# Sixteen products of ones ahead of the first scores, and a new order of the first 329 steps, in a fused attention and MLP kernel

## The chip, the cores and the metric

The kernel runs on one core of a Trainium2 chip. The core has five engines with a queue of instructions each, worked off in order: TensorE (PE in the profile) multiplies matrices, VectorE (DVE) and ScalarE (ACT) work on elements, GpSimd (POOL) does what is left, and SyncE (SP) issues the transfers between device memory and the core. An instruction that waits holds up everything behind it on its own engine, and nothing on the others. The metric is the time of one execution on the device in microseconds (us); the kernel before takes 593.65 us, the median of three runs from 591.35 to 593.74.

## The reference

An attention over a narrow band of keys and over block summaries, followed by a two-layer MLP with an exact GELU. There are 4 batches, 8 heads, 768 positions and a head size of 64:

```python
k_sum = k.reshape(B, H, nb, block, D).max(axis=3)        # block = 32
v_sum = v.reshape(B, H, nb, block, D).mean(axis=3)
scores_l = scale * np.matmul(q, k.transpose(0, 1, 3, 2))
mask_l = np.abs(pos[:, None] - pos[None, :]) < window    # window = 16
scores_s = scale * np.einsum('bhsd,bhnd->bhsn', q, k_sum) + np.log(block)
scores_all = np.concatenate([np.where(mask_l, scores_l, -1e9), scores_s], axis=-1)
a = np.exp(scores_all - np.max(scores_all, axis=-1, keepdims=True))
a = a / (np.sum(a, axis=-1, keepdims=True) + 1e-09)
x = np.matmul(a, np.concatenate([v, v_sum], axis=2))     # then (3072, 512)
h = x @ w_in                                             # (512, 2048)
out = (0.5 * h * (1 + erf(h / sqrt(2)))) @ w_out         # (2048, 512)
```

The attention's inputs are 32-bit floats; the two weights arrive as 64-bit floats.

## The kernel before, in words

**The work and its stages.** The attention is cut into 24 units, one for each batch, each third of the positions (256 queries) and each half of the heads (4). Two units make up a chunk of 256 rows for the MLP, so that there are 12 chunks. For the matrix products most operands are split into two 16-bit parts, "hi" and "lo", and three 16-bit products stand for one 32-bit product; units 0 to 5 do their attention in 32-bit products instead. Chunks from the fifth on compute the first layer with a Strassen scheme, and the last two chunks the second layer too.

**The order.** Nothing is planned at run time. The string `ORDER` lists 1653 steps by name, with the unit, chunk or weight block they work on; the kernel calls them one after the other, and each step appends its instructions to the queues of its engines. So the order of the list is the order on each engine's queue, SyncE's included, and instructions wait only where they need a result or a free buffer. The rest of this section names the steps that the change moves.

**The weights.** `fetch_w_in i` (line 346) brings a block of `w_in`, 1 MB of 64-bit floats. VectorE makes 32-bit floats of it by operations on bits, three to a block (`wi_bits`, lines 361, 366, 370), ScalarE the hi part (`wi_hi`, L396). The lo part comes either from VectorE (`wi_lo`, L399) or from TensorE, which subtracts by two products into PSUM (`wi_diff`, L407 and L408), and ScalarE copies it out (`wi_dlo`, L413). Block 5 also gets its Strassen differences early (`wt_add`, L424 and L430, on VectorE, then `wt_hi`, L435, on ScalarE and `wt_lo`, L438, on VectorE). `w_out` is treated alike (`wo_bits`, `wo_hi`, `wo_lo`).

**The keys and the block means.** `fetch_k b g` (L485) brings keys for the block maxima; `prep_k` (L494, VectorE) takes the maxima, `prep_k_end` (L502, L503) splits them, and `k_sums` (L507, ScalarE) spreads them. `sum_vt` (L521, TensorE) sums the values of batch 0 over blocks, and `mean_vt` (L528) copies the means out.

**One unit.** `load_q` (L566), `load_k`, `load_v` fetch. `k_pack` (L618, L620, ScalarE) lays keys and maxima side by side. `f_mask` (L607, TensorE) writes the mask into PSUM by four products, and `f_scores` (L631) adds 16 products of 32 bit to it, which the trace shows as 32 instructions. `evac` (L736, ScalarE) copies the scores out, `maximum` (L749, GpSimd) takes the largest over the partitions, `shift` (L754, VectorE) subtracts it, `exponent` (L757, ScalarE) follows, and TensorE makes the sums (`f_sums`, L653) and the values (`f_values`, L645). VectorE divides (`norm_take` L822, `norm_rec` L827 and L828, `norm_spread` L832, `norm_mult` L839), ScalarE takes the hi part (`x_hi`, L843) and VectorE the lo part (`x_lo`, L846). There is one PSUM buffer for scores and one for sums and values, one buffer for q, two for values, and four work buffers of 4 KB (tag `f4k`) which keys, scores, maxima and weights share.

**The MLP.** `phase1 c i` (L866 to L868, TensorE) multiplies chunk c with weight block i in 24 products; `gelu` (L875) and `g_hi` (L878) run on ScalarE, `g_lo` (L884) on VectorE; `phase2` (L983 to L985) multiplies with `w_out`. `phase1 0 ...` is the first step that needs both units of chunk 0, and `phase1 2 0` needs units 4 and 5.

## Time and profile before

| | |
|---|---|
| runs of the kernel before | 591.35, 593.65, 593.74 us (median 593.65) |
| the profiled execution | 591.23 us |
| its span, from the first instruction to the last | 589.4 us |
| TensorE busy | 570.1 us, 97% of the span |
| VectorE busy | 462.7 us, 78% |
| ScalarE busy | 360.6 us, 61% |
| GpSimd busy | 87.9 us, 15% |
| the chain of work that ended last, by engine | PE 86%, DVE 9%, DMA 2% |

A busy time is the time in which at least one instruction of the engine runs. Matmuls overlap in the pipeline, so a busy TensorE need not be at its peak rate: the spacing of the starts tells more than the duration of one. In a row of the timeline stand the start, the time that the group took, engine, line, operation, what is written and read, and in brackets the idle time ahead of it and what ended it. "SPq" is a transfer's issue on SyncE. Rows with "x32" stand for that many instructions.

### The profile page before, as it was taken

What the parts mean: (1) busy time and instruction counts of PE and PEld (TensorE: products, weight loads), DVE (VectorE), ACT (ScalarE), POOL (GpSimd) and SP (SyncE); (2) the same over time, 40 slices, a digit from 0 to 9 for tenths busy, and PEclk for the clock granted to TensorE, in tenths of its full rate; (3) what the DMA queues carried; (4) which work ended last, traced back from release to release, by engine and by line L of the source; (5) the groups of instructions that cost most, each with busy time, mean ns of one, the idle gap of its engine ahead of it and who ended that gap; (6) DMA issues with size and microseconds to landing.
All of it is one profiled execution on the core that took longest, in us unless ns stands there. A gap on an engine that the chain in (4) does not pass through costs nothing.

```text
span 589.4 us, 13159 instructions
## 1 busy us (share of the span) xinstructions
PE 570.1 (97%) x5676; PEld 389.8 (66%) x5676; DVE 462.7 (78%) x647; ACT 360.6 (61%) x533; POOL 87.9 (15%) x41
## 2 busy tenths in 40 slices
...
GB/s 282 360 311 294 297 171 181 232 183 153 156 67 142 86 77 136 72 128 77 126 30 94 98 82 94 57 62 34 80 40 10 14 19 19 2 19 18 1 1 72
DMA packets 28794, 64.49 MB, mean 109 GB/s; under 512 B 2752, under 2 KB 7616, under 8 KB 28736
## 3 DMA queue, kind: packets, MB, share of 16 engines
...
HBM read 55.58 MB, written 6.29 MB: 105 GB/s over the span
## 4 chain that ended last, share of the span: by engine, by line
PE 86%; DVE 9%; DMA 2%; ACT 1%; issue 1%; POOL 1%; SPq 0%; POOLq 0%; DVEq 0%; ACTq 0%
PE psy L937 15%; PE pso L983 12%; PE pso L984 12%; PE pso L985 12%; PE psz L937 7%; PE psx L937 4%; PE pso_y L1148 4%; PE psh L866 4%; PE psh L867 3%; PE psh L868 3%; PE psv L802 3%; PE pss L726 2%; PE pss_x L1148 2%; PE psv L815 2%; DMA w_out_l<-in_mask_dram 1%; DMA w_out_l<-in_kp_dram 1%
## 5 line engine op out<-in xcount | busy, mean ns | idle before, releaser
L749 POOL PARTITION_ALL_REDUCE m<-s x24 | 82.1, 3422 | 341.0 <-DVE s L740 149.8
L983 PE MATMUL pso<-w_out_h,gg 128*128 128x512 f16 x320 | 121.4, 379 | 0.0
L984 PE MATMUL pso<-w_out_l,gg 128*128 128x512 f16 x320 | 121.3, 379 | 0.0
L985 PE MATMUL pso<-w_out_h,gg 128*128 128x512 f16 x320 | 121.3, 379 | 0.0
L937 PEld LDWEIGHTS <-wt 128*128 128x128 f16 x768 | 74.1, 98 | 12.3 <-issue 0.8
L866 PE MATMUL psh<-xos,ww 128*128 128x256 f16 x256 | 70.6, 276 | 0.1
L867 PE MATMUL psh<-xos,ww 128*128 128x256 f16 x256 | 70.6, 276 | 0.0
L868 PE MATMUL psh<-xos,ww 128*128 128x256 f16 x256 | 70.6, 276 | 0.0
L937 PE MATMUL psy<-xos,wt 128*128 128x256 f16 x576 | 69.8, 273 | 0.0
L937 PEld LDWEIGHTS <-ww 128*128 128x128 f16 x576 | 55.4, 98 | 14.8 <-issue 2.9
L985 PEld LDWEIGHTS <-gg 128*128 128x128 f16 x320 | 31.3, 98 | 37.7
L948 ACT ACTIVATE ww<-psy 128x512 f32<-128x512 f32 x48 | 28.0, 590 | 45.7 <-PE psy L937 43.7
L983 PEld LDWEIGHTS <-gg 128*128 128x128 f16 x320 | 31.3, 98 | 33.0 <-issue 0.4
L984 PEld LDWEIGHTS <-gg 128*128 128x128 f16 x320 | 31.3, 98 | 31.9
L969 DVE SCALAR_TENSOR_TENSOR gg<-g,gg 128x512 f16<-128x512 f32 x48 | 34.4, 730 | 11.7 <-ACT gg L965 11.5
L955 DVE TENSOR_TENSOR g<-psz,ww 128x512 f32<-128x512 f32 x24 | 16.5, 688 | 29.1 <-PE psz L937 22.9
L754 DVE TENSOR_TENSOR s<-s,m 128x1024 f32<-128x1024 f32 x24 | 29.0, 1216 | 8.9 <-POOL m L749 8.9
L962 ACT ACTIVATE g<-g 128x512 f32<-128x512 f32 x36 | 22.2, 624 | 18.2 <-DVE g L955 18.1
L757 ACT ACTIVATE s<-s 128x1024 f32<-128x1024 f32 x24 | 25.3, 1055 | 9.1 <-DVE s L754 8.8
L866 PEld LDWEIGHTS <-ww 128*128 128x128 f16 x256 | 25.4, 99 | 7.2 <-issue 2.8
L965 ACT ACTIVATE gg<-g 128x512 f16<-128x512 f32 x48 | 29.4, 623 | 1.2 <-PE pso L984 0.4
L867 PEld LDWEIGHTS <-ww 128*128 128x128 f16 x256 | 25.3, 99 | 4.6 <-issue 0.5
...
## 6 DMA issues: line engine op xcount, KB each, us to landing
...
```

The costliest lines, as they stand in the source:

```text
L749: nc.gpsimd.partition_all_reduce(out_ap=self.m32, in_ap=self.s32, channels=P, reduce_op=bass_isa.ReduceOp.max)
L754: nc.vector.tensor_tensor(out=self.s32, in0=self.s32, in1=self.m32, op=ALU.subtract)
L866: nc.tensor.matmul(ph[:, e, :], wh, xh, start=(k == 0), stop=False)
L867: nc.tensor.matmul(ph[:, e, :], wh, xl, start=False, stop=False)
L868: nc.tensor.matmul(ph[:, e, :], wl, xh, start=False, stop=(k == NCC - 1))
L937: nc.tensor.matmul(ps[:, e, :], ws, xx, start=(first and e == 0 and k == 0 and m == 0), stop=(k == 1 and m == 2), skip_group_check=True,)
L965: nc.scalar.activation(g_part(o // 2, q, 0, slice(o % 2, 4, 2)), g32t[b, q, o], AF.Copy, scale=SC_G)
L969: nc.vector.scalar_tensor_tensor(out=g_part(o // 2, q, 1, fs), in0=g32t.pop((b, q, o)), scalar=SC_G, in1=g_part(o // 2, q, 0, fs), op0=ALU ...
L983: nc.tensor.matmul(p, gh, w_out_h[:, f, :], start=(f == 0), stop=False)
L984: nc.tensor.matmul(p, gh, w_out_l[:, f, :], start=False, stop=False)
L985: nc.tensor.matmul(p, gl, w_out_h[:, f, :], start=False, stop=(f == NFC - 1))
L1148: nc.tensor.matmul(ps[:, j, :], g, ww_, start=(first and e == 0 and k == 0), stop=(e == 1 and k == 2), skip_group_check=True,)
```

## The change

It has three parts. In `setup`, `ones` (128x64, 16 bit) is set to one first instead of fourth, and TensorE gets 16 products of `ones` with itself, each 64 outputs by 512 columns, into a PSUM buffer that nobody reads; they stand at the head of TensorE's queue. The first 329 steps of `ORDER` stand in a new order; they are the same steps, and from the 330th step on the list is the same. And `prep_k` and `f_scores` get conditions with which they can serve other settings: `f_scores` can start a PSUM buffer without a mask, and `prep_k` asks by unit which batch is done in 32 bit.

In the list, wrapped anew, the lines behind the 329th step differ only in where they break. They are left out here ("...").

```diff
@@ -68,167 +68,168 @@
 N_G32 = 4
 N_OT = 1
 L2 = 5
+N_FILL = 16
 
 ORDER = '''
-fetch_k 0 0, prep_k 0 0, prep_k_end 0 0, fetch_w_in 5 5, load_m16, load_q 2, k_pack 2, f_mask 2, f_scores 2, wi_bits 5
-0, wi_bits 5 1, wi_bits 5 2, wt_add 5 0, wt_add 5 1, fetch_vt 0, wi_hi 5, load_eye, load_ind, fetch_w_in 0 0, wi_lo 5,
-k_sums 0 0, sum_vt 0, wt_add 5 2, evac 2, maximum 2, f_mask 0, load_neg, wi_bits 0 0, wi_bits 0 1, k_pack 0, wt_hi 5,
-wt_lo 5, load_q 0, f_scores 0, wi_bits 0 2, fetch_vt 1, fetch_k 0 1, prep_k 0 1, sum_vt 1, prep_k_end 0 1, shift 2,
-evac 0, maximum 0, wi_hi 0, shift 0, exponent 0, k_pack 1, exponent 2, wi_diff 0 0, fetch_vt 2, wi_diff 0 1,
-fetch_w_in 3 3, f_mask 1, load_q 1, fetch_w_in 2 2, sum_vt 2, mean_vt, load_v 0, f_sums 0, wi_bits 3 0, fetch_w_in 4
-4, wi_bits 3 1, f_scores 1, load_q 3, wi_bits 3 2, norm_take 0, wi_hi 3, s_load_vs 0, wi_diff 3 0, wi_bits 2 0,
-wi_bits 2 1, wi_bits 2 2, evac 1, wi_dlo 3 0, load_v 1, norm_rec 0, wi_hi 2, norm_spread 0, f_values 0, norm_mult 0,
-maximum 1, fetch_w_in 7 3, wi_diff 2 1, f_mask 3, wi_dlo 0 1, wi_diff 3 1, k_pack 3, x_hi 0, wi_bits 4 0, wi_bits 4 1,
-wi_dlo 0 0, x_lo 0, shift 1, exponent 1, s_load_vs 1, f_scores 3, wi_bits 4 2, f_sums 1, wi_hi 4, fetch_w_in 1 1,
-wi_bits 7 0, load_v 2, wi_bits 7 1, evac 3, f_values 1, wi_diff 2 0, wi_dlo 2 0, norm_take 1, maximum 3, norm_rec 1,
-norm_spread 1, norm_mult 1, x_hi 1, wi_bits 7 2, fetch_k 1 1, load_k 4, f_mask 4, fetch_w_out 0 4, x_lo 1, wi_dlo 2 1,
-f_sums 2, norm_take 2, prep_k 1 1, fetch_k 1 2, phase1 0 5, wi_hi 7, phase1 0 2, gelu 0 2, load_vs 2, f_values 2,
-shift 3, wi_lo 7, norm_rec 2, load_q 4, wi_lo 4, exponent 3, phase1 0 0, norm_spread 2, k_pack 4, wo_bits 0 0, wi_bits
-1 0, norm_mult 2, wo_bits 0 1, wi_bits 1 1, wo_bits 0 2, gelu 0 0, fetch_w_in 6 2, g_hi 0 0, gelu 0 5, f_scores 4,
-load_v 3, load_vs 3, wi_dlo 3 1, load_k 5, wi_bits 6 0, x_hi 2, f_sums 3, prep_k 1 2, norm_take 3, phase1 0 3, load_v
-4, wo_hi 0, x_lo 2, fetch_v 1 1, wi_bits 1 2, norm_rec 3, wo_lo 0, fetch_w_out 1 5, wi_bits 6 1, evac 4, f_values 3,
-load_q 5, prep_v 1 1, g_hi 0 5, f_mask 5, norm_spread 3, gelu 0 3, wi_hi 1, wi_bits 6 2, g_lo 0 0, norm_mult 3,
-maximum 4, fetch_k 1 0, k_pack 5, prep_k 1 0, shift 4, phase1 0 7, gelu 0 7, wo_bits 1 0, fetch_w_out 2 4, g_hi 0 7,
-wi_diff 1 0, x_hi 3, x_lo 3, exponent 4, wo_bits 1 1, g_hi 0 3, g_lo 0 3, g_hi 0 2, load_vs 4, load_mask, f_scores 5,
-g_lo 0 5, load_k 6, s_k_hi 6, fetch_k 1 3, phase1 0 4, wo_bits 1 2, g_lo 0 2, gelu 0 4, k_lo 6, phase1 1 5, fetch_v 1
-2, wi_hi 6, gelu 1 5, f_sums 4, norm_take 4, g_hi 1 5, prep_k_end 1 0, norm_rec 4, g_hi 0 4, f_values 4, g_lo 1 5,
-load_q 6, prep_k 1 3, s_q_hi 6, wo_bits 2 0, phase1 1 2, wo_hi 1, wo_lo 1, fetch_w_out 3 5, q_lo 6, wi_dlo 1 0, g_lo 0
-7, prep_v 1 2, phase1 1 0, fetch_v 1 0, wi_diff 1 1, gelu 1 0, g_lo 0 4, evac 5, maximum 5, prep_v 1 0, k_sums 1 0,
-norm_spread 4, load_v 6, wo_bits 3 0, gelu 1 2, wi_lo 6, shift 5, phase1 1 7, gelu 1 7, phase1 1 3, g_hi 1 7, wi_dlo 1
-1, exponent 5, phase1 0 1, fetch_v 1 3, norm_mult 4, wo_bits 2 1, wo_bits 3 1, load_v 5, f_sums 5, g_lo 1 7, gelu 0 1,
-g_hi 0 1, wo_bits 2 2, wo_bits 3 2, wo_hi 3, phase1 0 6, wo_hi 2, scores 6, norm_take 5, prep_v 1 3, x_hi 4,
-fetch_w_out 4 4, g_lo 0 1, phase1 1 4, load_vs 5, g_hi 1 2, g_hi 1 0, gelu 1 4, g_hi 1 4, load_q 7, k_sums 0 1, wo_lo
-2, wo_lo 3, fetch_k 2 1, f_values 5, s_q_hi 7, norm_rec 5, wo_bits 4 0, load_v 8, x_lo 4, wo_bits 4 1, add_mask 6,
-maximum 6, wo_bits 4 2, norm_spread 5, prep_k 2 1, phase2 0 0, norm_mult 5, g_lo 1 2, gelu 0 6, g_hi 0 6, wo_hi 4,
-g_lo 1 0, load_vs 6, load_k 7, fetch_w_out 5 5, x_hi 5, x_lo 5, prep_k_end 1 1, phase1 1 1, fetch_w_out 6 4, shift 6,
-phase1 1 6, gelu 1 3, g_hi 1 3, gelu 1 6, wo_bits 5 0, q_lo 7, v_hi 6, load_q 8, wo_bits 5 1, g_lo 1 3, phase1 2 0,
-g_hi 1 6, exponent 6, wo_bits 6 0, k_sums 1 1, s_k_hi 7, phase2 0 2, g_lo 0 6, gelu 1 1, phase1 2 4, s_q_hi 8, load_vs
...
+fetch_k 0 0, prep_k 0 0, k_pack 2, fetch_w_in 5 5, load_q 2, load_m16, f_mask 2, prep_k_end 0 0, f_scores 2, wi_bits 5
+0, wi_bits 5 1, wi_bits 5 2, load_eye, wt_add 5 0, wt_add 5 1, wt_add 5 2, fetch_w_in 0 0, wi_hi 5, wi_lo 5, wt_hi 5,
+wi_bits 0 0, fetch_w_in 3 3, k_pack 0, wi_bits 0 1, k_sums 0 0, load_q 0, wt_lo 5, wi_bits 0 2, evac 2, load_neg,
+load_ind, fetch_k 1 1, prep_k 1 1, fetch_vt 0, f_mask 0, f_scores 0, wi_bits 3 0, wi_hi 0, wi_diff 0 1, maximum 2,
+wi_bits 3 1, shift 2, wi_diff 0 0, fetch_k 0 1, evac 0, prep_k 0 1, fetch_w_in 4 4, wi_bits 3 2, maximum 0, load_q 1,
+sum_vt 0, prep_k_end 0 1, f_mask 1, fetch_vt 1, k_pack 1, exponent 2, shift 0, exponent 0, wi_bits 4 0, wi_dlo 0 1,
+wi_bits 4 1, wi_bits 4 2, f_scores 1, evac 1, sum_vt 1, f_sums 0, fetch_vt 2, fetch_w_in 1 1, norm_take 0, wi_hi 4,
+wi_lo 4, sum_vt 2, f_mask 3, load_v 0, wi_hi 3, wi_diff 3 1, load_v 1, maximum 1, norm_rec 0, load_q 3, wi_bits 1 0,
+wi_dlo 0 0, shift 1, mean_vt, s_load_vs 0, f_values 0, wi_diff 3 0, k_pack 3, wi_bits 1 1, fetch_w_in 2 2, norm_spread
+0, norm_mult 0, load_v 2, fetch_k 1 0, wi_bits 1 2, load_vs 2, exponent 1, x_hi 0, s_load_vs 1, x_lo 0, f_scores 3,
+f_sums 1, wi_bits 2 0, wi_bits 2 1, wi_hi 1, norm_take 1, evac 3, f_values 1, wi_diff 1 0, prep_k 1 0, wi_dlo 3 1,
+f_mask 4, load_k 4, k_pack 4, wi_diff 1 1, norm_rec 1, norm_spread 1, norm_mult 1, maximum 3, x_hi 1, f_sums 2, wi_dlo
+3 0, wi_dlo 1 1, wi_bits 2 2, load_q 4, k_sums 0 1, x_lo 1, fetch_w_in 7 3, load_v 3, f_values 2, load_vs 3, shift 3,
+exponent 3, wi_bits 7 0, wi_bits 7 1, norm_take 2, norm_rec 2, f_scores 4, evac 4, wi_bits 7 2, norm_spread 2,
+norm_mult 2, wi_dlo 1 0, fetch_w_out 0 4, load_q 5, phase1 0 0, wi_hi 7, wo_bits 0 0, phase1 0 5, prep_k_end 1 0,
+wo_bits 0 1, f_sums 3, norm_take 3, gelu 0 0, fetch_w_in 6 2, maximum 4, f_values 3, phase1 0 1, shift 4, load_k 5,
+f_mask 5, norm_rec 3, gelu 0 5, g_hi 0 5, fetch_w_out 1 5, wi_bits 6 0, k_pack 5, f_scores 5, x_hi 2, wi_hi 2, wo_bits
+0 2, wi_lo 7, x_lo 2, g_hi 0 0, fetch_k 1 2, g_lo 0 0, wo_hi 0, gelu 0 1, wo_lo 0, wi_diff 2 0, load_v 4, g_hi 0 1,
+norm_spread 3, exponent 4, prep_k 1 2, wo_bits 1 0, wi_dlo 2 0, load_k 6, load_vs 4, load_q 6, fetch_k 2 1, norm_mult
+3, phase1 0 7, wo_bits 1 1, wi_bits 6 1, x_hi 3, x_lo 3, phase1 0 4, gelu 0 4, wi_bits 6 2, wi_hi 6, fetch_v 1 0,
+wo_bits 1 2, f_sums 4, norm_take 4, phase1 0 3, gelu 0 7, g_hi 0 7, wo_hi 1, prep_v 1 0, norm_rec 4, load_v 5, load_vs
+5, g_lo 0 1, fetch_w_out 2 4, gelu 0 3, g_hi 0 3, f_values 4, wo_lo 1, wo_bits 2 0, wi_lo 6, wo_bits 2 1, evac 5,
+prep_k 2 1, wo_bits 2 2, phase1 1 0, wi_diff 2 1, wi_dlo 2 1, load_v 6, fetch_w_out 3 5, fetch_v 1 1, s_k_hi 6, s_q_hi
+6, wo_hi 2, fetch_v 1 2, q_lo 6, k_lo 6, g_lo 0 3, g_lo 0 7, load_q 7, g_hi 0 4, load_k 7, wo_lo 2, phase2 0 0, g_lo 0
+4, k_sums 1 0, prep_v 1 1, norm_spread 4, gelu 1 0, g_hi 1 0, g_lo 1 0, phase1 0 2, gelu 0 2, norm_mult 4, phase1 1 3,
+prep_v 1 2, maximum 5, fetch_w_out 4 4, load_mask, gelu 1 3, fetch_v 1 3, shift 5, wo_bits 3 0, phase1 0 6, g_lo 0 5,
+g_hi 1 3, s_q_hi 7, wo_bits 3 1, g_lo 1 3, phase1 1 6, g_hi 0 2, exponent 5, scores 6, phase1 1 2, gelu 1 2, q_lo 7,
+g_lo 0 2, gelu 1 6, g_hi 1 6, g_hi 1 2, wo_bits 4 0, prep_v 1 3, f_values 5, wo_bits 3 2, wo_hi 3, f_sums 5, wo_bits 4
+1, phase1 1 5, load_vs 6, norm_take 5, x_hi 4, v_hi 6, fetch_w_out 5 5, wo_bits 4 2, wo_hi 4, gelu 1 5, fetch_k 1 3,
+norm_rec 5, phase1 1 7, x_lo 4, add_mask 6, wo_lo 3, gelu 0 6, g_lo 1 2, phase1 1 4, g_hi 0 6, phase1 1 1, gelu 1 7,
+norm_spread 5, norm_mult 5, prep_k 1 3, g_hi 1 7, x_hi 5, load_q 8, x_lo 5, g_hi 1 5, g_lo 1 7, maximum 6, shift 6,
+wo_bits 5 0, prep_k_end 1 1, gelu 1 4, g_hi 1 4, wo_bits 5 1, g_lo 1 5, phase1 2 0, exponent 6, load_v 8, fetch_w_out
+6 4, wo_bits 6 0, k_sums 1 1, s_k_hi 7, phase2 0 2, g_lo 0 6, gelu 1 1, phase1 2 4, s_q_hi 8, load_vs 8, g_lo 1 6,
...
@@ -318,11 +319,19 @@
         queue[0].dma_start(out=eye, in_=mask[:, NMT * TQ : NMT * TQ + P])
 
     def setup():
+        nc.gpsimd.memset(ones, 1.0)
+        if N_FILL:
+
+            fill = ps_h.tile([P, DM], F32, tag="psh", name="psh_fill")
+            for _ in range(N_FILL):
+                nc.tensor.matmul(
+                    fill[:D].rearrange("p (n d) -> p n d", d=D), ones, ones.unsqueeze(1).broadcast_to([P, DM // D, D]),
+                    start=True, stop=True,
+                )
         nc.gpsimd.memset(warm[:, 0:1], 1.0)
         nc.gpsimd.partition_all_reduce(
             out_ap=warm[:, 1:2], in_ap=warm[:, 0:1], channels=P, reduce_op=bass_isa.ReduceOp.max
         )
-        nc.gpsimd.memset(ones, 1.0)
         if N_F32:
             nc.gpsimd.memset(ones_f, 1.0 / SC_X)
             nc.gpsimd.memset(ks_f[:, :, NBLK:], 0.0)
@@ -486,7 +495,7 @@
         kst[b, g] = kt, rs
 
     def prep_k(b, g):
-        if b == 0 and N_F32:
+        if UPB * b < N_F32:
             ks32[b] = ks_f[:, :, :NBLK]
         if b not in ks32:
             ks32[b] = wk.tile([P, NPAIR, NBLK], F32, tag="ks32", name=f"ks32_{b}")
@@ -624,13 +633,16 @@
 
         def f_scores(self):
             kf = self.kf.rearrange("p r t j -> p (r t j)")
+            masked = self.pss is not None
+            if not masked:
+                self.pss = ps_s.tile([P, UCOLS], F32, tag="pss", name=f"pss_{self.nm}")
             for i in range(NR * CT):
                 kb = (i // CT * (CT + 1) + i % CT) * KW
                 for e in range(2):
                     rows = slice(e * D, (e + 1) * D)
                     nc.tensor.matmul(
                         self.pss[:, e * QCOLS + i * TQ : e * QCOLS + (i + 1) * TQ], kf[rows, kb : kb + P],
-                        self.q32[rows, i * TQ : (i + 1) * TQ], start=False, stop=(i == NR * CT - 1),
+                        self.q32[rows, i * TQ : (i + 1) * TQ], start=not masked, stop=(i == NR * CT - 1 or not masked),
                     )
 
         def f_values(self):
```

252 lines of the change are left out of this document (126 added, 126 removed).

## The prediction

> **What bounds the kernel now.** I read the page for the span, then busy time by stretch, then VectorE's groups with what ended their idle time, then the timeline of the first 30 us and of the end of the reordered part.
>
> ```profile
> span 589.4 us, 13159 instructions
> ```
> ```profile
> 0.00:111.03 111.03, 97.00 (x912) 67.84 (x913) 97.60 (x125) 71.09 (x101) 31.06 (x24) 0.98 0.78 270
> 111.03:589.40 478.37, 473.15 (x4764) 321.95 (x4763) 365.06 (x523) 289.53 (x433) 56.85 (x17) 1.00 0.24 72
> ```
> The columns after the stretch are its length, then TensorE's busy time, its weight loads, VectorE, ScalarE, GpSimd, granted clock, DMA share, GB/s. I cut at 111.03 because there `phase1 2 0` starts, the 327th of the 1653 steps; from the 330th step on the two orders are the same. Behind the cut TensorE is busy for 473.15 of 478.37 us: that part lasts as long as its products, and the change leaves them alone. So all that can be won lies ahead of the cut.
>
> ```profile
> 110.87 0.69 DVE L846 TENSOR_TENSOR xos<-x32s,xos 128x512 f16<-128x512 f32 x1
> 111.03 0.27 PE L866 MATMUL psh<-xos,ww 128*128 128x256 f16 x1
> ```
> What sets the cut? `phase1 2 0` reads unit 5's low half, which VectorE makes with `x_lo 5` (L846), ending at 111.56. The product that needs it is the seventh to ninth of this step, 0.7 us after 111.03. So TensorE arrives as VectorE delivers: VectorE sets the cut. Its idle time before it:
>
> ```profile
> L494 DVE TENSOR_REDUCE ks_f<-w_out_l 128x48 f32<-128x1536 f32 x2 | 3.5, 1754 | 6.7 <-DMA w_out_l<-in_kp_dram 6.7
> L754 DVE TENSOR_TENSOR s<-s,m 128x1024 f32<-128x1024 f32 x6 | 7.3, 1219 | 3.1 <-POOL m L749 3.1
> L438 DVE SCALAR_TENSOR_TENSOR wt<-t,wt 128x1024 f16<-128x1024 f32 x1 | 1.3, 1321 | 1.5 <-ACT wt L435 1.5
> L361 DVE TENSOR_SCALAR wt<-x32s 128x1024 int32<-128x1024 int32 x1 | 0.7, 694 | 0.5 <-DMA x32s<-in_w_in_dram 0.5
> L822 DVE STREAM_TRANSPOSE dent<-psv 128x512 f32<-128x512 f32 x6 | 4.3, 710 | 0.4 <-PE psv L645 0.4
> ```
> The last numbers are idle time and its releaser: 6.7 + 3.1 + 1.5 + 0.5 + 0.4 = 12.2 us. The rest of 111.56, 99.3 us, is work.
>
> **The change, part by part.** *No cost at all:* `prep_k`'s condition is true for the same batch as before (6 times 0 is below 6, 6 times 1 isn't), and `f_scores` keeps its old flags, since the new order still has an `f_mask` ahead of each of the six units that use it.
>
> *The order.* Ahead of `x_lo 5` VectorE has 114 steps (124 instructions) in either order; `g_lo 1 5` and `g_lo 1 7` move behind it, `g_lo 1 3` and `q_lo 7` ahead, all near 0.69 us. So its work stays 99.3 us, and the cut moves by what VectorE's idle time changes. Its first rows:
>
> ```profile
> 5.22 1.75 DVE L494 TENSOR_REDUCE ks_f<-w_out_l 128x48 f32<-128x1536 f32 x1 [5.22 <-DMA w_out_l<-in_kp_dram]
> 7.89 0.69 DVE L361 TENSOR_SCALAR wt<-x32s 128x1024 int32<-128x1024 int32 x1 [0.46 <-DMA x32s<-in_w_in_dram]
> 8.60 1.89 PE L607 MATMUL pss<-w_out_l 128*128 128x512 f16 x4 [8.60 <-DMA w_out_l<-in_mask_dram]
> 9.88 1.23 DVE L370 SCALAR_TENSOR_TENSOR wt<-x32s,wt 128x1024 int32<-128x1024 int32 x1
> 10.41 3.68 PE L631 MATMUL pss<-q,kf 64*128 64x64 f32 x32
> 11.14 1.06 ACT L396 ACTIVATE ww<-wt 128x1024 f16<-128x1024 f32 x1 [3.65 <-DVE wt L370]
> 11.14 0.69 DVE L424 TENSOR_TENSOR t<-wt 128x512 f32<-128x512 f32 x1
> 11.87 0.43 DVE L430 TENSOR_TENSOR t<-wt,t 128x256 f32<-128x256 f32 x1
> 12.11 0.34 ACT L507 ACTIVATE k_hi<-ks 128x192 f16<-128x192 f16 x1
> ...
> 14.13 0.33 SPq L566 DMA_DIRECT2D q<-in_qd_dram  x1
> 14.14 1.02 ACT L736 ACTIVATE s<-pss 128x1024 f32<-128x1024 f32 x1 [1.44 <-PE pss L631]
> 14.98 0.43 SPq L485 DMA_DIRECT2D w_out_l<-in_kp_dram  x1
> 15.26 3.59 POOL L749 PARTITION_ALL_REDUCE m<-s  x1 [13.28 <-ACT s L736]
> 15.26 0.73 ACT L618 ACTIVATE kf<-w_out_l 128x640 f32<-128x640 f32 x1
> 15.89 0.41 ACT L620 ACTIVATE kf<-ks_f 128x256 f32<-128x256 f32 x1
> 16.20 1.04 ACT L435 ACTIVATE wt<-t 128x1024 f16<-128x1024 f32 x1
> 17.44 1.03 PE L607 MATMUL pss<-w_out_l 128*128 128x512 f16 x4
> 18.40 2.00 PE L631 MATMUL pss<-q,kf 64*128 64x64 f32 x32
> 18.52 1.21 DVE L370 SCALAR_TENSOR_TENSOR wt<-gg,wt 128x1024 int32<-128x1024 int32 x1
> 20.33 1.95 PE L521 MATMUL psh_vt<-w_out_h,w_out_l 128*88 128x512 f32 x4
> 21.18 1.75 DVE L494 TENSOR_REDUCE ks_f<-w_out_l 128x48 f32<-128x1536 f32 x1 [1.45 <-DMA w_out_l<-in_kp_dram]
> 22.12 1.02 PE L407 MATMUL psw<-wt,eye 128*128 128x512 f32 x2
> 26.08 1.06 ACT L757 ACTIVATE s<-s 128x1024 f32<-128x1024 f32 x1 [3.66 <-DVE s L754]
> 27.28 1.08 PE L653 MATMUL psv<-s,ones_f 128*64 128x512 f32 x4 [0.27 <-ACT s L757]
> ```
> What stays: 5.22 for the first keys (still the first transfer) and 0.46 for the first weight, 5.7 us. The other 12.2 - 5.7 = 6.5 us go as follows.
>
> 1.5 (`wt_lo 5`, L438): ScalarE's `wt_hi 5` (L435) comes right behind `wi_hi 5`, at about 12.8 to 13.8, and VectorE has two weight steps in between. Gone.
>
> 1.45 (second keys, L494 at 21.18): these were issued at 14.98, behind a `load_q 0` that waits on SyncE's queue until TensorE has read q of unit 2. VectorE's work ahead of that wait ended at 18.52 + 1.21 = 19.73; in the new order the very same set stands ahead of `prep_k 1 1`, and without the 1.5 it ends at 18.2. Its transfer again stands behind `load_q 0`. With TensorE fast (below) that goes out at 12.1. From 7.89, at the stretch from 5 to 10 us's rate
>
> ```profile
> 5.00:10.00 5.00, 1.40 (x4) 0.43 (x4) 4.19 (x6) 1.15 (x2) 0.00 (x0) 1.00 1.05 398
> ```
> the 2.7 MB ahead (q, mask, eye, two weights by the shapes) end at 14.6, q, indicator and keys (0.8 MB) at 16.7: 1.5 us to spare. At TensorE's slow rate q goes out at 14.7. The old keys took 6.2 us from issue to landing with 1.6 MB in front and of their own (4.0 at this rate), so 2.2 on top; that gives 18.9, a wait of 0.7.
>
> 3.1 (`shift 5`, L754):
> ```profile
> 86.23 1.03 ACT s L736
> 87.40 3.51 POOL m L749
> ```
> Unit 5's scores were copied only at 86.23, and VectorE had 3.6 us of work between `evac 5` and `shift 5` to cover the copy and the 3.5 us maximum. Now 10.3 us of VectorE's steps stand there. Gone; if something delays `evac 5` by over 5 us, it is back. 0.4 (`norm_take 1`): gone or not, I count it as gone.
>
> So the most is 6.5. *New waits.* On ScalarE `evac 2` now stands behind `wi_hi 5`, `wt_hi 5` (to 13.8), `k_pack 0` (0.73 + 0.41) and `k_sums` (twice 0.34): 15.6 to 16.6 instead of 14.14. The maximum lasts to 20.3; `shift 2` is due at 18.2 + 0.9 + 0.7 + 1.3 = 21.1. No wait. But behind `evac 2` stands all of TensorE: `f_mask 0` needs its buffer, and `sum_vt 0`, which filled this place before, has moved behind. TensorE ends `f_scores 2` at 12.1 to 14.7 and is idle until 16.6. From there to `norm_take 0` it has two masks (0.9 each), two scores (2.0 each), two `wi_diff` (1.02 for two, with the third product some 1.1), two `sum_vt` (1.8 each): 11.6 us, to 28.2 at the full rate; the exponent, `shift 0` at 26.0 plus 1.22 plus 1.06, allows 28.3; `f_sums 0` ends at 29.4. VectorE comes to `norm_take 0` at 30.2 (26.0, `shift 0`, three weight steps of 0.7, 1.2, 1.2). It has 0.8 us to spare, for as long as TensorE is fast.
>
> *TensorE's rate* is what can't be read off. The rows show two: four L607 in 1.89, later in 1.03; 32 L631 in 3.68, later in 2.00. TensorE was slow for 8.75 us of work, from 8.60 to the fast row at 17.44 (the granted-clock column does not show this first slow stretch). It was slow once more:
>
> ```profile
> 75.37:78.78 3.41, 1.25 (x34) 1.20 (x35) 3.32 (x10) 3.37 (x7) 0.00 (x0) 1.00 0.70 210
> 78.78:82.20 3.42, 3.42 (x18) 2.43 (x17) 3.42 (x6) 1.79 (x3) 0.00 (x0) 0.50 0.71 234
> ```
> A stretch with 1.25 us of products in 3.41 is followed by 3.42 us at a granted clock of 0.50. The new idle stretch, 1.9 to 4.5 us long, is at least about as empty, so I expect a slow stretch of L us somewhere after 16.6. It costs L/2, and VectorE waits L/2 - 0.8 at `norm_take 0`. Bounds: L = 0 (no wait), 3.4 (0.9), 8.75 as at the start (3.6). I take 5.6, in between, since the scores that follow did not end the slow rate at 10.41 to 14.0 either: 2.0 us.
>
> *The fill products.* `ones` is set first on GpSimd, so they start near 1 us; 16 of 512 columns at the slow row's 0.43 us take 6.9, at the fast 0.22 some 3.5. They end by 8 us. The mask, now behind q, lands near 9.2 (256 KB later than 8.60), so nothing waits for them. By the 8.75 us of the trace they are too short to change the rate by themselves; then `f_scores 2` ends at 14.7 and the price is the 0.7 us above. At the fast rate it ends at 9.2 + 0.9 + 2.0 = 12.1. I take the fast rate, which the trace does not prove; both ends are in the range.
>
> [...]
>
> **Sum.** 6.5 - 2.0 = 4.5 us off the cut at 111.03, and so off the end, because the order behind is unchanged and VectorE and TensorE both come earlier by the same. The profiled execution took 591.23 us, 1.8 more than its span: 586.7. It stands 2.4 below the median of the runs, 593.65; against that, which I forecast: **589.1**. Own range 587.1 (no wait) to 591.
>
> **Rivals.** *The wait only moves (0.25).* Slow for the full 8.75 (3.6), and SyncE's queue on top: `fetch_k 1 0` stands behind `load_v 2`, which waits for `f_values 0` (end near 35.5). If it lands 6.2 us after its issue near 36.4, like the old keys, VectorE, due at 41.0, waits 1.6: 5.2 in all, 592.4. For: these queues delayed L494 once already. Against: at 398 GB/s its 0.9 MB and 2.2 us land at about 41.
>
> *Slower (0.13).* The slow rate does not end before unit 0's sums. The wait L/2 - 0.8 passes 6.5 from L = 14.6 on; at L = 22 it is 10.2, and the time 597.4. For: 30 scores kept TensorE busy from 10.5 to 13.9 without a faster rate. Against: it came once the four L521 had run, and the new order puts products of that kind, L407 and L521, right behind `f_scores 0`.
>
> *The fill does nothing (inside the forecast).* It costs 0.7 us more, 589.8; the order alone is then the gain.
>
> **Chances.** Forecast, with its rivalless best, 0.61; the wait moves 0.25; slower 0.13; 0.01 for the rest. Half a per cent, 3.0 us, is about what a measurement here can tell from no change. Faster than 590.7 takes new waits below 3.5: 0.61; within: 0.26; slower: 0.13. The range goes from 585 (all 6.5 off the profiled execution's time) to 594.5, which holds the moved wait and leaves out most of the slower case.
>
> **What would show it.** `x_lo 5` should end at 105 to 109 instead of 111.56, with VectorE's idle time ahead of it at 6 to 9 us; L438's and L754's waits gone; TensorE idle for 2 to 4.5 us ahead of the second L607, at about 16.6, and behind it L631 in over 2.0 us; the wait of the first L822 on L653. Wrong would be idle time over 12 us before `x_lo 5`, a transfer among its releasers, or TensorE behind 111 us no longer continuous.

## The result, and the profile after

The changed kernel is slower: 595.4 us, the median of 18 runs (592.7 to 597.61), against 591.49 us for 18 runs of the kernel before beside them (589.74 to 594.57). The ratio is 1.0059, with a 95% interval of 1.0043 to 1.0076. The forecast was 589.1 us. The profiled execution took 596.01 us.

I cut the profile after where the prediction cut the one before, at the start of `phase1 2 0` (116.03 instead of 111.03), and read the busy time by stretch. The columns are those of the prediction: length, then TensorE, its weight loads, VectorE, ScalarE, GpSimd, granted clock, DMA share, GB/s.

```profile
116.03:594.20 478.17, 472.99 (x4766) 321.91 (x4763) 363.91 (x522) 288.18 (x431) 56.74 (x17) 1.00 0.23 70
```

Behind the cut nothing has changed: 478.17 us instead of 478.37. All that was lost lies ahead of it. The next two rows, the same view of the kernel after and of the kernel before, run to the end of `x_lo 5`, which the prediction took for what sets the cut.

```profile
0.00:115.46 115.46, 102.92 (x923) 70.22 (x924) 102.30 (x126) 70.55 (x100) 29.71 (x24) 0.93 0.78 267
```
```profile
0.00:111.56 111.56, 97.53 (x917) 68.31 (x918) 98.13 (x126) 71.62 (x102) 31.06 (x24) 0.98 0.78 271
```

`x_lo 5` ends 3.90 us later. VectorE runs 125 instructions in both (the view counts one more, just begun), of the same usual lengths, yet it is busy for 102.30 us instead of 98.13: 4.17 us more for the same work. The rest, in which it isn't busy, is 13.16 us instead of 13.43. So the idle time that the new order was expected to take away is nearly all still there, and the work has become longer.

**The idle time.** VectorE's groups of the kernel after up to 115.5 us, with busy time, mean ns of one, idle time ahead and its releaser (lines 370 to 503 are 361 to 494 of the kernel before, L834 is L822, L552 is `prep_v`):

```profile
L552 DVE TENSOR_REDUCE vs<-vb 96x32 f32<-96x1024 f32 x4 | 4.8, 1199 | 1.9 <-DMA vb<-in_vb_dram 1.9
L503 DVE TENSOR_REDUCE ks<-kp 128x24 f32<-128x768 f32 x5 | 4.7, 931 | 0.7 <-DMA kp<-in_kp_dram 0.7
L834 DVE STREAM_TRANSPOSE dent<-psv 128x512 f32<-128x512 f32 x6 | 4.3, 711 | 3.3 <-PE psv L665 3.2
L503 DVE TENSOR_REDUCE ks_f<-w_out_l 128x48 f32<-128x1536 f32 x2 | 3.5, 1749 | 5.0 <-DMA w_out_l<-in_kp_dram 5.0
L685 DVE TENSOR_TENSOR ql<-q,qh 128x512 f16<-128x512 f32 x2 | 1.4, 686 | 0.6 <-ACT qh L676 0.6
L370 DVE TENSOR_SCALAR wt<-x32s 128x1024 int32<-128x1024 int32 x1 | 0.7, 694 | 0.5 <-DMA x32s<-in_w_in_dram 0.5
```

5.0 + 0.5 are the two waits that had to stay. The old waits at `wt_lo 5` (1.5) and `shift 5` (3.1) are gone. In their place stand 3.3 at `norm_take 0`, 1.9 for a transfer of values (`prep_v 1 1`), 0.7 for the second keys and 0.6 at `q_lo 6`: 12.0 in all, against 12.2.

**The clock.** The same kernel's busy time in stretches of the length in which its granted clock (the third column from the end) steps:

```profile
3.40:6.95 3.55, 3.55 (x10) 1.45 (x9) 1.88 (x2) 0.80 (x2) 0.00 (x0) 1.00 1.04 407
6.95:10.36 3.41, 1.79 (x11) 0.65 (x11) 2.83 (x5) 0.35 (x1) 0.00 (x0) 1.00 1.06 384
10.36:13.78 3.42, 1.76 (x32) 1.72 (x31) 3.32 (x6) 1.09 (x2) 0.00 (x0) 1.00 1.05 388
13.78:17.19 3.41, 0.00 (x0) 0.00 (x0) 3.38 (x4) 3.41 (x7) 0.00 (x0) 0.50 1.03 353
17.19:20.60 3.41, 3.40 (x20) 2.00 (x19) 2.70 (x4) 1.22 (x2) 3.36 (x1) 0.50 1.00 384
20.60:24.02 3.42, 3.42 (x22) 2.54 (x21) 3.39 (x3) 1.30 (x2) 0.99 (x2) 0.50 0.65 227
24.02:27.43 3.41, 3.41 (x6) 1.36 (x5) 3.38 (x5) 1.70 (x3) 3.04 (x1) 0.50 0.97 349
27.43:30.84 3.41, 3.41 (x24) 1.64 (x24) 3.34 (x4) 1.54 (x2) 0.00 (x0) 1.00 1.05 402
```

(The 1.00 in the first row is not to be read: the column shows a half rate only after the first change.) The rate opened at 6.95, as hoped: the products of ones start 0.43 us apart up to 6.91, the mask's products from 9.15 on 0.22. TensorE then had gaps, and from 13.78 to 27.43 the clock was at a half: 13.65 us, of which it had products from 17.2 on. (It was at a half once more, from 47.91 to 51.33.) The timeline of the kernel after (start, time, engine, line, and idle time ahead in brackets) shows these products, and what VectorE and GpSimd did beside each other:

```profile
0.94 6.59 PE L327 MATMUL psh_fill<-ones 128*64 128x512 f16 x16 [0.94 <-POOL warm L331]
9.15 1.04 PE L616 MATMUL pss<-w_out_l 128*128 128x512 f16 x4 [1.62 <-DMA w_out_l<-in_mask_dram]
9.71 1.22 DVE L379 SCALAR_TENSOR_TENSOR wt<-x32s,wt 128x1024 int32<-128x1024 int32 x1
10.12 2.00 PE L643 MATMUL pss<-q,kf 64*128 64x64 f32 x32
16.15 1.00 ACT L748 ACTIVATE s<-pss 128x1024 f32<-128x1024 f32 x1
17.20 1.87 PE L616 MATMUL pss<-w_out_l 128*128 128x512 f16 x4 [5.08 <-ACT s L748]
19.00 3.68 PE L643 MATMUL pss<-q,kf 64*128 64x64 f32 x32
23.84 3.22 POOL L761 PARTITION_ALL_REDUCE m<-s  x1 [2.43 <-ACT s L748]
24.24 2.57 DVE L379 SCALAR_TENSOR_TENSOR wt<-gg,wt 128x1024 int32<-128x1024 int32 x1
...
33.72 1.08 PE L665 MATMUL psv<-s,ones_f 128*64 128x512 f32 x4
34.85 0.72 DVE L834 STREAM_TRANSPOSE dent<-psv 128x512 f32<-128x512 f32 x1 [3.24 <-PE psv L665]
...
43.59 1.03 POOL L598 COPY v<-w_out_h 24x1024 f32<-24x1024 f32 x1 [7.24 <-DMA v<-in_vw_dram]
43.65 2.06 DVE L375 SCALAR_TENSOR_TENSOR wt<-gg,wt 128x1024 int32<-128x1024 int32 x1
...
108.25 1.06 ACT L786 ACTIVATE vh<-v 128x1024 f16<-128x1024 f32 x1 [0.63 <-DMA v<-vm]
110.79 0.27 PE L878 MATMUL psh<-xos,ww 128*128 128x256 f16 x1 [1.52 <-ACT g L887]
```

**The longer work.** L379 (`wi_bits`, third part) takes 1.22 us by itself, as at 9.71; at 24.24, beside GpSimd's maximum, it takes 2.57. L375 takes 2.06 beside GpSimd's copy of the block means (`load_vs`, L598). If each VectorE instruction is compared with the usual duration of its form, those beside GpSimd's work are 5.6 us too long in the kernel after, up to `x_lo 5`, and 1.2 us in the kernel before. The difference is about the 4.2 us of the busy time. Of the 5.6 us, 4.0 stand beside the maxima and 1.6 beside the copies.

**TensorE's own sum.** The start of `phase1 2 0` is also the time that TensorE spent on the products of ones, on the 912 other products ahead of it, and without work. In the kernel before that was 97.0 us of products and 14.0 without work; in the kernel after it was 6.6 of ones, 96.9 of products and 12.5 without work. The ones run where TensorE had stood at the start anyway: the mask's products begin at 9.15 instead of 8.60, 0.55 us later. Behind that point TensorE stood for 5.4 us before and for 10.0 after: 5.08 at 17.20, 2.52 at 46.43, 0.86 at 63.57 and 1.52 at 110.79. These 4.6 us and the 0.55 are the whole loss of 5.0, less 0.1 of products.

So at the cut TensorE did not meet `x_lo 5`. The product that needs it comes 0.7 us behind 116.03, and `x_lo 5` had ended at 115.46. What TensorE met was the gelu ahead of 110.79, which stood on ScalarE behind `v_hi 6` (L786); that step waited for a transfer of block means that VectorE had finished at 104.87.

### The profile page after: what moved, and what is told of

It is laid out like the page before. It is cut to its first block, busy times and chain, and to the rows that moved or that the text cites. A ratio compares the mean times of both kernels' runs of the same rounds, so it can differ in the third digit from the quotient of the medians.

```text
span 594.2 us, 13192 instructions
## 1 busy us (share of the span) xinstructions
PE 576.5 (97%) x5692; PEld 392.6 (66%) x5692; DVE 466.8 (79%) x647; ACT 358.7 (60%) x531; POOL 86.7 (15%) x41
## 4 chain that ended last, share of the span: by engine, by line
PE 86%; DVE 8%; DMA 3%; ACT 1%; issue 1%; SPq 0%; DVEq 0%; ACTq 0%
PE psy L949 14%; PE pso L995 12%; PE pso L997 11%; PE pso L996 11%; PE psz L949 7%; PE psx L949 4%; PE pso_y L1160 4%; PE psh L878 3%; PE psh L880 3%; PE psh L879 3%; PE psv L814 3%; PE pss L738 2%; PE pss_x L1160 2%; DMA vb<-in_vb_dram 2%; PE psv L827 2%; PE pss L643 1%
## 5 line engine op out<-in xcount | busy, mean ns | idle before, releaser
L878 PE MATMUL psh<-xos,ww 128*128 128x256 f16 x256 | 69.9, 273 | 1.5 <-ACT g L887 1.5
L880 PE MATMUL psh<-xos,ww 128*128 128x256 f16 x256 | 69.8, 273 | 0.0
L879 PE MATMUL psh<-xos,ww 128*128 128x256 f16 x256 | 69.8, 273 | 0.0
```

Source lines behind the costliest of these rows:

```text
L878: nc.tensor.matmul(ph[:, e, :], wh, xh, start=(k == 0), stop=False)
L879: nc.tensor.matmul(ph[:, e, :], wh, xl, start=False, stop=False)
L880: nc.tensor.matmul(ph[:, e, :], wl, xh, start=False, stop=(k == NCC - 1))
```

## The experiments

My theory after this profile: the cut is VectorE's idle time plus VectorE's work, and the work lengthens beside GpSimd's maxima and copies; the new order wins idle time and loses it to longer instructions, and the slow clock behind the gap takes the rest. The rival: the clock alone. TensorE's sum above speaks against the first part of this theory; the experiments come back to it. All medians stand beside 16 to 29 runs of the kernel before on the same chip; each is of 11 to 18 runs, that of experiment 8 of 6.

**1. The products alone.** The old order, with the 16 products ahead of it.

```diff
+N_FILL = 16
...
+        nc.gpsimd.memset(ones, 1.0)
+        if N_FILL:
+            fill = ps_h.tile([P, DM], F32, tag="psh", name="psh_fill")
...
-        nc.gpsimd.memset(ones, 1.0)
```

> The old order with the 16 products of ones alone. My theory (the fill works, and what it opens is lost in the new order only because TensorE then stands idle): TensorE is at its full rate from about 7 us, the first scores end near 11.5 instead of 14.1 us, the q of unit 0 and the second keys go out 2.6 us earlier, so that VectorE's waits of 1.45 us (second keys) and most of 1.5 us (L438) go; the sums over v fill TensorE's place behind the scores, so the rate holds. x_lo 5 ends 2 to 3 us earlier, the time is 2 to 3 us below the kernel before. Rival (the fill is useless, or itself the harm): within 0.5 us of the kernel before, or above it.

Measured: 588.91 us, ratio 0.9956 (0.9935 to 0.9977). One of the two parts is a gain of 2.6 us by itself. How it comes about the profile does not show: that execution took 592.26 us, the longest of the twelve, and `x_lo 5` ended at 112.62 in it, not 2 to 3 us earlier but 1.1 later than before.

**2. The order alone.** The changed kernel with no products.

```diff
-N_FILL = 16
+N_FILL = 0
```

> The new order without the 16 products. My theory (the loss comes from the order): the first scores end near 14.7 us at half rate, the keys for prep_k 1 1 come 2 us later than in the changed kernel (its wait grows from 0.7 to about 2 us), the rate is still half at the second scores, and the wait at norm_take 0 is about as long as the changed kernel's 3.2 us, or shorter by what VectorE comes later. The time is 0 to 2 us above the changed kernel. Rival (the fill is the harm): 3 to 4 us below the changed kernel, as the kernel before.

Measured: 594.15 us, ratio 1.0038 (1.0009 to 1.0067). The order is the part that loses. In its profile (598.54 us, 4.4 above the median) the clock opened at 27.11, where that of the kernel before opened at 17.35, so the gap costs the order the clock even without the products; with them the median is 1.2 us higher still (595.4), which the two intervals don't separate.

**3. Products in the gap.** The changed kernel with 20 more products of ones right behind the first scores.

```diff
-... prep_k_end 0 0, f_scores 2, wi_bits 5 0,
+... prep_k_end 0 0, f_scores 2, fill 20, wi_bits 5 0,
```

> The changed kernel with 20 more products of ones (4.3 us at the full rate) right behind the first scores, where TensorE stands idle from 12.1 to 17.2 us. My theory (the idle stretch loses the clock, and the slow 13.6 us make VectorE wait at norm_take 0): no half rate from 13.8 to 27.4 us, the second scores end near 20 instead of 22.7 us, the wait of 3.2 us at norm_take 0 falls below 1 us, the time is 2 to 3.5 us below the changed kernel, near the kernel before. Rival (the clock does not matter, the time is lost elsewhere): within 0.7 us of the changed kernel.

Measured: 593.52 us, ratio 1.0025 (1.0002 to 1.0049). Its busy time by stretch, while the clock was open and up to `phase1 2 0`, and two of VectorE's groups (L387 and L378 are the third and the first part of `wi_bits`):

```profile
0.00:112.52 112.52, 103.11 (x948) 70.89 (x949) 104.48 (x127) 70.58 (x100) 31.74 (x24) 0.97 0.78 276
5.05:42.60 37.55, 30.83 (x235) 16.47 (x233) 35.77 (x39) 22.52 (x31) 12.43 (x4) 1.00 0.96 352
```
```profile
L387 DVE SCALAR_TENSOR_TENSOR wt<-gg,wt 128x1024 int32<-128x1024 int32 x6 | 9.0, 1495 | 0.0
L378 DVE TENSOR_SCALAR wt<-gg 128x1024 int32<-128x1024 int32 x6 | 5.7, 946 | 0.0
```

The clock stayed open from 5.05 to 42.60, the wait at `norm_take 0` was gone, and VectorE was not busy for only 8.0 us ahead of the end of `x_lo 5` (13.4 before). That gain of 5.4 us in idle time is what the prediction looked for. But VectorE was busy for 103.9 us instead of 98.1, so `x_lo 5` ended at 111.91, 0.35 us later than before. With the clock open behind the first scores the new order still gains nothing. That does not rule the clock out: it was at a half from 42.60 to 49.43, after TensorE had stood for 3.04 us ahead of 43.49, and the median is 1.9 us below that of the changed kernel, with intervals that meet.

**4. What GpSimd does to VectorE.** A kernel of its own, which computes nothing of the reference: runs of one kind of VectorE instruction, first alone, then beside one maximum of 128x1024, then beside one copy of 24x1024.

```python
for f, n in ((ts, 8), (stt, 5), (tt, 5), (lo, 5), (red, 4), (cast, 14), (tr, 8), (pm, 8)):
    for _ in range(n): f()
    mark(s32); nc.gpsimd.partition_all_reduce(out_ap=m32, in_ap=s32, channels=P, reduce_op=bass_isa.ReduceOp.max)
    for _ in range(n): f()
    mark(vm); nc.gpsimd.tensor_copy(out=v32[64:88, :], in_=vm[64:88, :])
    for _ in range(n // 2 + 1): f()
```

> A kernel of its own that computes nothing of the reference and writes zeros or ones: VectorE repeats eight kinds of its instructions alone, then beside the maximum over partitions on GpSimd, then beside GpSimd's copy of 24x1024. My theory (GpSimd's work holds up certain kinds of VectorE's instructions): the integer kind with one input (0.69 us), the kinds with two inputs in SBUF (1.22 us) and the cast are longer by 0.6 to 1.4 us in total beside the maximum, and one instruction by about 0.85 us beside the copy; the reduction, the transpose out of PSUM and the product with an input in PSUM keep their times. Rival (the longer instructions in the changed kernel came from transfers or from the instructions' places): none is longer.

Measured, in the timeline of this kernel:

```profile
10.47 6.33 DVE L48 TENSOR_SCALAR bits<-raw 128x1024 int32<-128x1024 int32 x8
16.83 8.44 DVE L48 TENSOR_SCALAR bits<-raw 128x1024 int32<-128x1024 int32 x8
17.07 4.01 POOL L99 PARTITION_ALL_REDUCE m<-s  x1 [5.93 <-DVE s L78]
...
29.66 6.26 DVE L54 SCALAR_TENSOR_TENSOR bits<-raw,bits 128x1024 int32<-128x1024 int32 x5
35.96 7.83 DVE L54 SCALAR_TENSOR_TENSOR bits<-raw,bits 128x1024 int32<-128x1024 int32 x5
36.19 4.08 POOL L99 PARTITION_ALL_REDUCE m<-s  x1 [9.30 <-DVE s L78]
...
85.27 7.11 DVE L66 TENSOR_REDUCE mx<-kt 128x48 f32<-128x1536 f32 x4
92.70 7.12 DVE L66 TENSOR_REDUCE mx<-kt 128x48 f32<-128x1536 f32 x4
92.84 3.22 POOL L99 PARTITION_ALL_REDUCE m<-s  x1 [9.82 <-DVE s L78]
...
132.69 5.77 DVE L75 TENSOR_TENSOR stage<-psv,dent 128x512 f32<-128x512 f32 x8
138.49 5.77 DVE L75 TENSOR_TENSOR stage<-psv,dent 128x512 f32<-128x512 f32 x8
```

One maximum makes the run of `wi_bits`' first kind 2.11 us longer, that of its other kinds (two inputs in SBUF) 1.57, and itself 0.8 to 0.9 longer (3.22 to 4.01 or 4.08). A reduction (7.11 and 7.12 us for four), or a product whose first input lies in PSUM (5.77 both times for eight), leaves the maximum at 3.22 and is not slowed; neither is the transpose out of PSUM (5.96 and 5.97 us for eight). Fourteen casts of 128x48 go from 3.09 to 5.77 us. The copy counts too: beside it three instructions with two inputs in SBUF take 4.46 us, where three fifths of 6.26 are 3.76, and it takes 1.92 itself instead of 1.03. So the price of a maximum or a copy depends on which VectorE instruction stands beside it. In these rows each loses time to the other, but VectorE's run is only 1.57 us longer beside a maximum of 4.08: it does not stand still for the whole of it. How the two divide that time is not shown.

**5. The maxima taken away.** The kernel of experiment 3 with GpSimd's maxima of units 0 to 5 cut down to 8 columns.

```diff
+            n = 8 if self.u < 6 else UCOLS
-                out_ap=self.m32, in_ap=self.s32, channels=P, ...
+                out_ap=self.m32[:, :n], in_ap=self.s32[:, :n], channels=P, ...
...
-            nc.vector.tensor_tensor(out=self.s32, in0=self.s32, in1=self.m32, op=ALU.subtract)
+            m32 = self.s32 if self.u < 6 else self.m32
+            nc.vector.tensor_tensor(out=self.s32, in0=self.s32, in1=m32, op=ALU.subtract)
```

> The new order with products of ones in the gap behind the first scores, and for units 0 to 5 GpSimd's maximum over 1024 columns cut to its first 8 columns; the shift subtracts the scores from themselves, one VectorE instruction of the same size, so that part of the softmax is left out. With the whole maxima this kernel had 6.9 us of VectorE's idle time ahead of x_lo 5, of which none at a shift, 7.35 us by which VectorE's instructions ran longer than alone, and x_lo 5 ended at 111.91; 5.8 of the 7.35 stood beside the maxima and 1.8 beside the copies of load_vs. Contention theory: the lengthening falls to 1 to 2.5, x_lo 5 ends at 105.5 to 107.5, and the time falls by 4 to 6 from 593.5, to 587.5 to 589.5. Rival (the longer instructions have another cause, or TensorE's own order holds the cut): the lengthening or the time stays, 592 to 594.

Measured: 590.19 us, ratio 0.9971 (0.9949 to 0.9992). Busy time to the end of `x_lo 5`, and three of VectorE's groups (L560 is `prep_v`, L844 `norm_take`):

```profile
0.00:109.24 109.24, 99.72 (x943) 68.88 (x944) 96.87 (x126) 70.97 (x100) 13.34 (x24) 1.00 0.82 281
```
```profile
L387 DVE SCALAR_TENSOR_TENSOR wt<-gg,wt 128x1024 int32<-128x1024 int32 x6 | 7.2, 1207 | 0.0
L560 DVE TENSOR_REDUCE vs<-vb 96x32 f32<-96x1024 f32 x4 | 4.8, 1200 | 2.4 <-DMA vb<-in_vb_dram 2.4
L844 DVE STREAM_TRANSPOSE dent<-psv 128x512 f32<-128x512 f32 x6 | 4.3, 711 | 1.7 <-PE psv L673 1.7
```

VectorE's busy time fell from 103.87 to 96.87 us, by 7.0; L387 fell from 1495 to 1207 ns; no instruction ran long any more. That settles that the longer work comes from what GpSimd does beside it, in the main from the maxima: in experiment 3, some 5.5 us of it stood beside them and 1.8 beside the copies, which now met other instructions and lengthened none. Of the 7.0 us only 2.7 reached the end of `x_lo 5`, and 3.3 the time, less than I expected: VectorE, now earlier, waited 2.4 us for values and 1.7 for sums that had been hidden before. TensorE's sum tells it in another way. It stood as long as in experiment 3 (9.5 and 9.4 us), but its products took 90.4 us instead of 93.0, because the clock stayed open all through (1.00 in the first row above). The waits of 1.15 at 35.09 and 3.04 at 43.49 had shrunk to 0.17 and 1.64, and one of 2.01 for a gelu was new, at 104.60.

**6. Two waits of the old order.** The kernel of experiment 1 with `shift 1` one weight step earlier and 3.1 us of VectorE's work ahead of `shift 5`.

```diff
-wi_bits 4 0, wi_bits 4 1, wi_dlo 0 0, x_lo 0, shift 1, exponent 1,
+wi_bits 4 0, shift 1, wi_bits 4 1, wi_dlo 0 0, exponent 1, x_lo 0,
...
-wi_lo 6, shift 5, ..., norm_mult 4, wo_bits 2 1, wo_bits 3 1, load_v 5
+wi_lo 6, norm_mult 4, wo_bits 2 1, wo_bits 3 1, shift 5, ..., load_v 5
```

> The old order with 16 products of ones, and two moves in VectorE's list: shift 1 one weight step earlier (ahead of wi_bits 4 1, and its exponent ahead of x_lo 0), and norm_mult 4, wo_bits 2 1 and wo_bits 3 1 (3.1 us) ahead of shift 5. Theory (VectorE's idle time sets the cut): the waits of 1.71 at norm_take 1 and 3.12 at shift 5 go, x_lo 5 ends at 107 to 109 instead of 112.6, phase1 2 0 starts at 108.5 to 110 because TensorE's own gaps shrink by 3 at the most, and the time is 585 to 587.5 (588.9 without the moves). Rival (TensorE is the bound there already, the waits only move to f_sums 5 and norm_take 5): 588 to 589.5.

Measured: 592.95 us, ratio 1.0022 (1.0002 to 1.0041). None of it came. In its profile (594.91 us, the longest of the twelve) the wait at `shift 5` is gone, but other waits (1.3 at the shifts, 2.4 behind the values of a unit, 1.3 for a transfer of values) and another meeting with GpSimd have come: VectorE is busy for 102.98 us up to `x_lo 5`, against 101.17 without the moves.

**7. The copies on ScalarE.** The kernel of experiment 3, with the copies of the block means of units 2 and 3 taken from GpSimd.

```diff
-wi_bits 1 2, load_vs 2, exponent 1, ... x_hi 1, f_sums 2, ... f_values 2, load_vs 3, shift 3, exponent 3, wi_bits 7 0
+wi_bits 1 2, exponent 1, ... x_hi 1, s_load_vs 2, f_sums 2, ... f_values 2, shift 3, exponent 3, s_load_vs 3, wi_bits 7 0
```

> The new order with the products in the gap, and the copies of the block means of units 2 and 3 done by ScalarE instead of GpSimd. They lengthened the wi_bits beside them by 0.72 and 0.84. Contention theory: these two go, x_lo 5 ends 1 to 1.6 us earlier than 111.91 unless another instruction takes their place beside GpSimd, and the time is 592 to 593. Rival (ScalarE's copies hold up an exponent): 593.5 to 595.

Measured: 591.86 us, ratio 1.0019 (0.9994 to 1.0044). The two longer `wi_bits` are gone and VectorE's busy time fell from 103.87 to 101.21, but the ratio can't be told from experiment 3's 1.0025. In this profile the clock fell back once more, early:

```profile
6.21:9.62 3.41, 1.39 (x8) 0.46 (x6) 2.84 (x5) 0.42 (x1) 0.00 (x0) 1.00 1.06 387
9.62:13.03 3.41, 3.41 (x27) 2.57 (x25) 3.27 (x6) 1.06 (x1) 0.00 (x0) 0.50 1.04 386
```

The 16 products end near 7.5 and the mask comes at 9.2; a stretch with 1.39 us of products was enough.

**8. The gap closed by the order.** The changed kernel with `evac 2` right behind the first scores on ScalarE, without products in the gap.

```diff
-f_scores 2, wi_bits 5 0, ... wi_bits 0 2, evac 2, load_neg,
+f_scores 2, evac 2, wi_bits 5 0, ... wi_bits 0 2, load_neg,
```

> The changed kernel with evac 2 moved ahead of wi_hi 5 on ScalarE, right behind the first scores, so that TensorE's gap of 5.1 us shrinks to some 1.3 us without any product in it. Theory: the clock stays open, the wait of 3.24 at norm_take 0 goes, VectorE's idle time falls from 12.0 to 6.5 to 8.5, but the lengthening beside GpSimd stays at 5 to 8; x_lo 5 ends at 110.5 to 113 and the time is 591.5 to 594. Rival (the lengthening came from where the slow clock had put the maxima): 587 to 590. Rival (the gap does not matter): 595.

Measured: 597.98 us (6 runs), ratio 1.0105 (1.0076 to 1.0133), the slowest of all; none of the three expectations. The clock had opened at 3.68 in its profile and fell back at 10.51, ahead of the first scores' end, by the gap between the products and the mask as above; it stayed at a half until 27.57. `evac 2` now held up `wi_hi 5` behind it, and VectorE waited 3.0 us at `wi_lo 5`. So the small gap ahead of the mask can cost the clock as well. Here the stretch up to 10.51 held 1.28 us of products. In the kernel after the stretch at that place held 1.79 (6.95 to 10.36), and the clock stayed open behind it. One profile of each does not show how often it falls.

**9 and 10. A longer fill, and a transfer moved.** Experiment 9 is the kernel of experiment 7 with 26 products at the head:

```diff
-N_FILL = 16
+N_FILL = 26
```

Experiment 10 is the same with the late transfer of values ahead of two others:

```diff
-load_v 6, fetch_w_out 3 5, fetch_v 1 1,
+fetch_v 1 1, load_v 6, fetch_w_out 3 5,
```

> The kernel with products in the gap and ScalarE's copies, with 26 instead of 16 products at the head, so that TensorE does not stand still between their end (7.5) and the mask's products (9.2). In the profile with 16 the rate opened at 6.21, fell back from 9.62 to 16.45, the first scores took 3.68 us and VectorE waited 1.79 and 0.91 behind them. Theory: the rate stays open from 4 to 7 us on, these two waits shrink by 1.5 to 2.5 together, x_lo 5 ends at 107.5 to 109.5 instead of 110.65, and the time is 589 to 591 (591.86 with 16). Rival (the longer fill delays the mask's products and the scores behind it as much as it gains): 591.5 to 593.

> The same with fetch_v 1 1 moved ahead of load_v 6 and fetch_w_out 3 5 on SyncE's queue. In the changed kernel this transfer was issued at 83.17, right behind these two, landed at 93.47, and VectorE waited 1.92 for it; load_v 6 itself waits for the values of unit 4. Theory: the transfer lands 2 us or more before VectorE needs it, the wait is gone wherever it was left, and the time is 0 to 2 below the kernel without the move, 588 to 590.5. Rival (its buffer comes free no earlier, and it holds up load_v 6 and the weight behind it): 0.5 to 2 above it.

Measured: 591.66 us, ratio 0.9991 (0.9969 to 1.0014), and 591.57 us, ratio 0.9990 (0.9975 to 1.0006). With a fill that reaches to the mask the early fall of the clock is gone from both profiles (up to the cut the granted clock is 0.98 in both, 0.95 in experiment 7; each has one of 3.41 us later, at 29.05 and at 43.41). By the medians that is worth no more than 0.2 us, which the intervals don't separate. The new order comes out even with the kernel before, no better. The transfer made no difference: with the clock open VectorE didn't wait for it in either.

**11 and 12. The old order again.** Experiment 11 has 26 products instead of 16, the line changed as in experiment 9. Experiment 12 has 16, and of experiment 6 only the second move:

```diff
-wi_lo 6, shift 5, ..., norm_mult 4, wo_bits 2 1, wo_bits 3 1, load_v 5
+wi_lo 6, norm_mult 4, wo_bits 2 1, wo_bits 3 1, shift 5, ..., load_v 5
```

> The old order with 26 instead of 16 products at the head. In the old order 16 were enough: TensorE had other work behind them and the rate opened at 4.47. Theory: no difference beyond 0.3 per cent from 588.9, 587.5 to 590; VectorE's idle time ahead of x_lo 5 is 9.5 to 10.5 and its lengthening beside GpSimd 3 to 5. Rival (the fill delays the first scores, which VectorE's second keys wait for behind load_q 0): 590 to 592.

> The old order with 16 products of ones, and of the two moves only the second: norm_mult 4, wo_bits 2 1 and wo_bits 3 1 (3.1 us of VectorE's work) ahead of shift 5. Nothing changes before 86 us. Theory: VectorE's wait of 3.1 at shift 5 goes, x_lo 5 ends 2 to 3 us earlier than without the move, TensorE's gap of 1.5 us ahead of phase1 2 0 closes, and the time falls by 1 to 2 from 588.9 to 590.8 (the same order with 16 and with 26 products), to 587 to 589.5. Rival (another wait takes its place, at prep_v 1 3 or norm_take 5, as with both moves, or a longer instruction beside the maximum of unit 5): 589.5 to 592.

Measured: 590.75 us, ratio 0.9986 (0.9966 to 1.0006), and 588.82 us, ratio 0.9955 (0.9938 to 0.9973). The first has a higher ratio than with 16 products (0.9956), though the intervals meet; its early steps are not later, but one weight step at 60.9 ran 1.69 us long beside a maximum. Whether that is usual in its runs stays open. The second can't be told from experiment 1 in time. In its profile (L374 is the second part of `wo_bits`, L551 `prep_v`) the 3.1 us at `shift 5` are gone, and part of them came back at once:

```profile
83.00 5.17 POOL L757 PARTITION_ALL_REDUCE m<-s  x1 [16.65 <-ACT s L744]
85.59 2.32 DVE L374 SCALAR_TENSOR_TENSOR wst<-xos,wst 128x1024 int32<-128x1024 int32 x1
...
94.76 1.22 DVE L551 TENSOR_REDUCE vs<-vb 96x32 f32<-96x1024 f32 x1 [1.08 <-DMA vb<-in_vb_dram]
```

1.10 us as a longer instruction beside the maximum, which itself took 5.17 instead of 3.22, and 1.08 as a wait for values. Both this kernel and that of experiment 1 beat the kernel before and the changed one.

**All profiles in one sum.** In every profiled execution I read the end of `x_lo 5`, VectorE's busy time up to it (125 instructions each time), the start of `phase1 2 0`, and the execution's own time:

| profile | `x_lo 5` ends | busy | not busy | `phase1 2 0` | time | time less start |
|---|---|---|---|---|---|---|
| before | 111.56 | 98.13 | 13.43 | 111.03 | 591.23 | 480.20 |
| after | 115.46 | 102.30 | 13.16 | 116.03 | 596.01 | 479.98 |
| 1, products alone | 112.62 | 101.17 | 11.45 | 112.10 | 592.26 | 480.16 |
| 2, order alone | 115.12 | 100.92 | 14.20 | 118.54 | 598.54 | 480.00 |
| 3, products in the gap | 111.91 | 103.87 | 8.04 | 112.52 | 592.51 | 479.99 |
| 5, without the maxima | 109.24 | 96.87 | 12.37 | 109.83 | 589.81 | 479.98 |
| 6, old, both moves | 114.65 | 102.98 | 11.67 | 114.91 | 594.91 | 480.00 |
| 7, copies on ScalarE | 110.65 | 101.21 | 9.44 | 111.54 | 591.58 | 480.04 |
| 8, `evac 2` early | 116.01 | 104.32 | 11.69 | 117.10 | 597.07 | 479.97 |
| 9, 26 products | 109.62 | 101.18 | 8.44 | 110.52 | 590.71 | 480.19 |
| 10, and the transfer | 110.47 | 102.85 | 7.62 | 111.36 | 592.27 | 480.91 |
| 11, old, 26 products | 110.59 | 100.17 | 10.42 | 110.06 | 590.26 | 480.20 |
| 12, old, one move | 108.62 | 100.23 | 8.39 | 108.10 | 588.28 | 480.18 |

The last column is the same within 1 us thirteen times: the time is decided ahead of the cut. One profile is one execution: that of experiment 1 took 592.26 where the median is 588.91. With products in the gap and the whole maxima, the new order brings the time in which VectorE isn't busy from 13.4 to between 7.6 and 9.4, and its busy time from 98 to between 101 and 104. How much longer VectorE's work was in the executions that were not profiled is not shown.

For five of these profiles, TensorE's sum up to the start of `phase1 2 0`:

| profile | products of ones | other products | without work | `phase1 2 0` |
|---|---|---|---|---|
| before | 0 | 97.0 | 14.0 | 111.03 |
| after | 6.6 | 96.9 | 12.5 | 116.03 |
| 3, products in the gap | 10.2 | 93.0 | 9.4 | 112.52 |
| 5, without the maxima | 9.9 | 90.4 | 9.5 | 109.83 |
| 12, old, one move | 5.3 | 91.8 | 11.0 | 108.10 |

## Why the prediction was wrong

**What held.** The part behind the cut did not change, and the first scores ended at 12.12 for a forecast of 12.1. The fast rate that this forecast takes was the author's choice; the kernel after shows it from 6.95 on, and the scores' 32 instructions in 2.00 us. `evac 2` ran from 16.15 for a forecast of 15.6. The waits at `wt_lo 5`, `shift 5` and `norm_take 1` went as said, 5.5 us of the 5.7 stayed, and the second keys waited 0.7, the slow-rate value. The new wait came where it was put, at the first L834 on the sums.

**The step that failed** is "So its work stays 99.3 us, and the cut moves by what VectorE's idle time changes." Neither half held.

*The work.* (The view has 98.13 us of it; the rest of the 99.3 is short gaps.) The number of instructions and their kinds stayed, their durations did not: 4.2 us more busy time up to `x_lo 5` in the kernel after, 5.7 in experiment 3, and -1.3 without the maxima. The prediction took a duration from one row and moved it elsewhere in time, beside work of GpSimd for which these instructions don't wait. No rival held this either. That GpSimd's maxima cause most of it, and its copies the rest, is shown by experiments 4, 5 and 7.

*The cut.* The prediction read off one row that TensorE arrives as VectorE delivers. The whole stretch ahead of that row says more, first of the kernel before, then of experiment 3:

```profile
77.53:111.03 33.50, 33.39 (x347) 26.33 (x348) 30.25 (x41) 21.30 (x34) 8.51 (x3) 0.95 0.59 198
```
```profile
61.75:112.52 50.77, 50.77 (x542) 40.91 (x543) 50.03 (x66) 36.80 (x53) 9.14 (x4) 1.00 0.71 241
```

In the kernel before TensorE had products without a break from 77.53 on. Only the one at 111.03 came late: it started 0.39 us behind the one ahead of it, where those ahead follow at 0.11. So an idle time of VectorE behind 77.53, the 3.1 us at `shift 5` above all, could bring the cut forward by some 0.3 us at the most, as long as TensorE's own products and earlier waits stayed. Experiment 12 agrees: it takes these 3.1 us out of the kernel of experiment 1, and the time can't be told from that kernel's. In experiment 3 VectorE's idle time is 5.4 us smaller, but the cut 1.5 later, and TensorE has no break from 61.75 to the cut. The 5.08 us gap ahead of the second mask, which the prediction expected at 1.9 to 4.5 us and priced only by what VectorE would wait, is a wait of TensorE itself. The prediction has no sum of TensorE's products and waits; with it the 3.1 us, at least, would not have stood as a gain.

**The term that was mis-sized** is L, the length of the slow stretch: 5.6 us was taken, the longest bound was 8.75, and the clock was at a half for 13.65. TensorE had products only from 17.2 on, so 10.2 us of it counted; by the prediction's formula, L/2 - 0.8, that is 4.3. The wait was 3.24, because VectorE itself came to `norm_take 0` at 31.6 instead of 30.2. The bound was taken from the 8.75 us of slow work at the start, where four L521 came right behind the first scores; in the new order a second set of 32-bit scores came first (19.00 to 22.68). That such scores do not open the clock is read from the rows, not tested. What was said for the slower rival, that the 32-bit scores keep TensorE busy without a faster rate, is what happened, though the half rate ended ahead of unit 0's sums. That a slow stretch would come at all, which the prediction took from the half rate behind 78.78, was right: in the gap of 5.08 us the clock fell to a half, at 13.78, and in experiment 3, which closes the gap, the wait is gone.

**The term that was missed** on the side of the idle time are two late releases at unit 6 and batch 1, 0.6 and 1.9. The transfer of values was issued at 83.17 behind two others and landed 10.3 us later. In experiments 3, 9 and 10, without the early slow stretch, they are 0.4 and 0.2 or less. But in experiment 5, where the clock never fell, the wait for the values is 2.4, so the slow stretch alone does not explain it; the cause stays open. A transfer among the releasers was one of the signs of being wrong that the prediction had named, and it came.

**The sum again.** The prediction: 6.5 gone, 2.0 new, 4.5 us earlier. Measured at `x_lo 5`: of the 6.5, the second keys kept 0.7, so 5.8 with the 0.2 of the first waits on top is 6.0 gone; 3.3 + 1.9 + 0.6 = 5.8 new; 4.2 of longer work. That is 4.0 us later, and the profile shows 3.9. By the executions' own times it is 4.8, because TensorE came to `phase1 2 0` another 1.1 us later: the gelu had held it for 1.52 us at 110.79. How the loss divides between the slow stretch and the longer work is not settled. Closing the gap is worth 1.9 us by the medians of the changed kernel and of experiment 3, whose intervals meet. Taking the maxima away as well brings 3.3 more; of the 2.7 us between the two profiles, 2.6 are TensorE's products at a clock that no longer fell. With both gone, experiment 5 lies 1.7 us below the kernel before by its ratio, where 4.5 had been forecast. The longer work can't be what is missing there, since VectorE was busy for only 96.87 us. The base was off too: 593.65 us was the median of three runs, that of 18 is 591.49, and 4.5 below that is 587.0.
